# Transposing attention's result by DMA instead of TensorE for six of sixteen tiles of a fused attention and MLP block

## The chip, the cores and the metric

The kernel runs on one core of a Trainium2 chip. Its metric is the device time of one execution in microseconds (us); a time is the median of several runs. The core's engines each run their own queue of instructions in order: TensorE (PE in the profile, with its weight loads as PEld), VectorE (DVE), ScalarE (ACT), GpSimd (POOL) and SyncE (SP), which here mostly issues DMA transfers. They wait for each other by semaphores.

## What is computed

One transformer block in fp32 on a sequence of 2048 positions with 512 features: layer norm, attention with 32 heads of 16 features over a dilated window (8 keys, two positions apart), output projection and residual; then layer norm, an MLP with 1792 hidden features and squared ReLU, and residual.

```python
def _A_ref(x, wqkv, wo):
    qkv = (x @ wqkv).reshape(B, S, 3, H, Dh) ...
    idx = pos[:, None] - off[None, :]          # off = 0, 2, ..., 14
    logits = einsum("bhsd,bhswd->bhsw", q, k[idx]) * Dh ** -0.5
    attn = softmax(where(idx >= 0, logits, -1e9))
    o = einsum("bhsw,bhswd->bhsd", attn, v[idx])
    return o.transpose(0, 2, 1, 3).reshape(B, S, D) @ wo

def _B_ref(x, w1, b1, w2, b2):
    h = x @ w1 + b1
    r = where(h > 0, h, 0)
    return (r * r) @ w2 + b2

h = x + _A_ref(_layernorm(x), wqkv, wo)
h2 = h + _B_ref(_layernorm(h), w1, b1, w2, b2)
```

## The kernel before

**Tiles and groups.** The 2048 positions are 16 tiles of 128 positions, one per partition. Four tiles (R = 4) make a group, two (RI = 2) a sub-group of the attention. Tile t belongs to group t // 4 and to sub-group t // 2. Every fp32 matrix product is made of three products of parts: a number is split into a high part (a copy in the reduced fp32r type, made by ScalarE in `hi`, L141) and a low part (the difference, made by VectorE or GpSimd in `lo`, L144), and high x high, low x high and high x low are summed in PSUM.

**Phases.** A first phase makes q, k and v for all tiles and stores them in a scratch tensor in DRAM, and prepares group 0. Then come three loops, u = 0, 1, 2, each of which runs the MLP of group u and, woven into it, the preparation of group u + 1. A last stage runs the MLP of group 3 in another form.

**A loop's slots.** A loop has 17 slots, p = 0 to 16. In slot p TensorE computes one block of 128 hidden features of the four tiles (`mlp1`, 12 matmuls, L224) and the second product of the block of three slots before (`mlp2`, 12 matmuls, L808). The hidden block goes from PSUM through ScalarE (ReLU L784, square L785, high part `rh` L141) and GpSimd or VectorE (low part `rl` L144) before `mlp2` uses it. In loop 0 each slot also loads one block of w2, splits it (`big_h`, `big_l`) and stores its low half to DRAM (`stash`); in loops 1 and 2 low halves are fetched back (`fetch`).

**Preparation of a tile of the next group.** For tile t = 4(u + 1) + i, tables give the slots: LH loads the residual row h; OP = 6, 7, 12, 13 is the slot of `o_T`; WP = 8, 9, 13, 14 (one earlier for i = 2, 3 in loop u = 2) that of the product with wo. `o_T` runs at the slot's start: four TensorE transposes of 128 x 128 against an identity (`tr<-ident,o`, L199) into one PSUM bank, and at the slot's end the high part `oh` by ScalarE and the low part `ol` by VectorE, both read from PSUM. `wo_product` makes 12 matmuls (`wo<-wo_h,oh` and so on, L224); then `h_add` adds the residual and takes the statistics (VectorE L577, L152, L153), GpSimd computes the norm's scale (`rs`, L158 to L162), ScalarE normalizes (`hn`, L194), GpSimd adds b2 (L587) and SyncE stores h. At the loop's end, slots 15 and 16 (halves of slots 14 and 15 in loop 2), `hn` of the four tiles is transposed by TensorE (`tr<-ident,hn`, L199); the next loop's first product needs all four.

**Attention.** The attention of a sub-group is a generator of steps: VectorE multiplies q with a window of k (`dots`, L335) and sums (L369), ScalarE copies q to PSUM (`qp`, L264) and exponentiates (`ex`, L392), VectorE weighs v (`weigh`, L346), GpSimd adds up the products in a tree into `o` (L403). Its k, v and q windows are loaded by SyncE (L243, L256).

**Order.** The program text is emitted in one pass, and each engine runs its own instructions in the order of emission. A planner keeps two estimated clocks, one for TensorE and one for VectorE. At each slot's end `end_slot` adds the slot's TensorE time, runs the chores due (`at`), draws attention steps from the generator (`pump`) until VectorE's clock has caught up, and runs the late chores (`after`). `pump(until=s)` draws steps until sub-group s is done. Row buffers of 2 KB per partition come from one shared pool of ROWS = 15, taken in turn; a new user waits for the last reader of the old one.

Of the kernel before, what the change touches and what calls it, by code (L numbers as in the profile page):

```python
# [7 lines left out]

F32 = mybir.dt.float32
F32R = mybir.dt.float32r  # L10
AF = mybir.ActivationFunctionType
ALU = mybir.AluOpType
X = mybir.AxisListType.X

S, D, H, DH, W, F = 2048, 512, 32, 16, 8, 1792
P = 128
KB = D // P
FB = F // P
R = 4
RI = 2  # L20
# [17 lines left out]
W2 = (18,)  # L38
LH = 3, 4, 10, 11
OP = 6, 7, 12, 13  # L40
WP = 8, 9, 13, 14
HP = 15, 15, 16, 16
UP = 14, 14, 15, 15
HL = (14, 0), (14, 1), (15, 0), (15, 1)
# [8 lines left out]
def block_kernel(ctx, tc, x, wqkv, wo, w1, b1, w2, b2, out):  # L53
    nc = tc.nc
# [31 lines left out]

    big_h = wpool.tile([P, 3 * KB, D], F32R, name="big_h")
    big_l = wpool.tile([P, 3 * KB, D], F32R, name="big_l")
    wq_h, wq_l = [t.rearrange("p (k c) n -> p k (c n)", k=KB) for t in (big_h, big_l)]
    wo_h = wpool.tile([P, KB, D], F32R, name="wo_h")  # L90
    wo_l = wpool.tile([P, KB, D], F32R, name="wo_l")
    w1_h = wpool.tile([P, KB, F], F32R, name="w1_h")
    w1_l = wpool.tile([P, KB, F], F32R, name="w1_l")
    w2_h, w2_l = {}, {}

    def row(name, shape=(P, D), dt=F32):
        return work.tile(list(shape), dt, name=name, tag="row", bufs=ROWS)
# [8 lines left out]
    def at(delta, fn, *a):  # L106
        due.setdefault(now["slot"] + delta, []).append((fn, a))
# [11 lines left out]
    def run(chores):  # L119
        todo = chores.get(now["slot"], [])  # L120
        while todo:
            fn, a = todo.pop(0)
            fn(*a)

    def dve(t):
        now["dve"] += t
# [13 lines left out]
    def hi(dst, src):  # L140
        nc.scalar.copy(dst, src)  # L141

    def lo(eng, dst, src, h):
        eng.tensor_tensor(out=dst, in0=src, in1=h, op=ALU.subtract)  # L144
# [3 lines left out]
    def norm_stats(key, src, delay=True):  # L148
        st = small.tile([P, 6], F32, name="st")
        mv = small.tile([P, 2], F32, name="mv", bufs=4)  # L150
        rs = small.tile([P, 2], F32, name="rs", bufs=4)
        nc.vector.bn_stats(st, src)  # L152
        nc.vector.bn_aggr(mv, st)  # L153
        dve(0.93)
        stats[key] = mv, rs

        def finish():
            nc.gpsimd.tensor_scalar(out=rs[:, 1:2], in0=mv[:, 1:2], scalar1=EPS, scalar2=None,  # L158
                                    op0=ALU.add)
            nc.gpsimd.tensor_tensor(out=rs[:, 0:1], in0=rs[:, 1:2], in1=mhalf, op=ALU.pow)  # L160
            if delay:
                nc.gpsimd.tensor_scalar(out=rs[:, 1:2], in0=mv[:, 0:1], scalar1=rs[:, 0:1],  # L162
                                        scalar2=-1.0, op0=ALU.mult, op1=ALU.mult)
        if delay:
            after(0, finish)
        else:
            finish()

    def act_stats(key, src):
# [4 lines left out]
        scrap = row("scrap")  # L174
        nc.scalar.activation(scrap, src, AF.Identity, accum_out=nm[:, 0:1])
        nc.scalar.activation(nm[:, 1:2], nm[:, 0:1], AF.Identity, scale=-1.0 / D)
        nc.scalar.activation(scrap, src, AF.Square, bias=nm[:, 1:2], accum_out=sq)
        stats[key] = nm, rs
# [8 lines left out]
    def norm_apply(key, dst, src, eng):  # L187
# [5 lines left out]
        else:  # L193
            nc.scalar.activation(dst, src, AF.Identity, scale=rs[:, 0:1], bias=rs[:, 1:2])  # L194

# [7 lines left out]
    def parts(tr, dst):  # L203
        n = len(dst)
        return [(dst[i], tr[:, i * KB // n:(i + 1) * KB // n]) for i in range(n)]

    def hi_T(tr, h_dst):
        for d, src in parts(tr, h_dst):
            hi(d, src)

    def lo_T(tr, h_dst, l_dst):
        for (d, src), h in zip(parts(tr, l_dst), h_dst):
            lo(nc.vector, d, src, h)
            dve(0.16 + 0.53 / len(h_dst))
# [16 lines left out]
    o_t = {}  # L231
# [35 lines left out]
    def attention():  # L267
# [39 lines left out]
        for n in range(N + 1):  # L307
# [77 lines left out]
            if new:  # L385
# [5 lines left out]
                yield 0.42 + 0.15 * ng  # L391
                nc.scalar.activation(lf, lf, AF.Exp, scale=DH ** -0.5)  # L392

# [4 lines left out]
    def add_up(p2, o, c0, s):  # L398
        w = W // 2
        while w:  # L400
            dst = p2[:, :, :w] if w > 1 else o[:, :, c0:c0 + GC].rearrange(
                "p i (w h d) -> p i w h d", w=1, h=GH)
            nc.gpsimd.tensor_tensor(out=dst, in0=p2[:, :, :w], in1=p2[:, :, w:2 * w], op=ALU.add)  # L403
            w //= 2
        done[s] += 1
# [3 lines left out]
    def pump(until=None):  # L409

        while (done[until] < G) if until is not None else (now["dve"] < now["pe"]):
            todo = sums[:]
            sums.clear()
            t = next(stream, "end")
            for a in todo:
                add_up(*a)
            if t == "end":
                now["dve"] = 1e9
                return
            if t is None:  # L420
                now["dve"] = max(now["dve"], now["pe"])
                return
            dve(t * SLOW[min(now['sub'] + 1, 2)])
# [128 lines left out]
    oT = {}  # L552
# [9 lines left out]
    def o_T(t):  # L562
# [9 lines left out]
        at(0, hi_T, tr, [oT[t][0]])  # L572
        at(0, lo_T, tr, [oT[t][0]], [oT[t][1]])

    def h_add(t, ps):
        h = hs[t]
        nc.vector.tensor_tensor(out=h, in0=ps, in1=h, op=ALU.add)  # L577
        dve(0.7)
        norm_stats(t, h)
# [168 lines left out]
    def products_b(n):  # L748
# [6 lines left out]
        tt = nc.vector.tensor_tensor  # L755
        nc.scalar.activation(rf[:, :HD], b[1], AF.Relu, bias=b1_sb[:, f:f + 1])
        tt(out=u[:, HD:], in0=b[2], in1=p[:, :HD], op=ALU.add)
# [131 lines left out]
    for n in range(16):  # L889
        gp, t = divmod(n, 4)  # L890
# [66 lines left out]
    def load_w2(f):  # L957
        raws[f] = row("raw2")
        nc.sync.dma_start(raws[f], w2[f * P:(f + 1) * P, :])
# [37 lines left out]
    for u in range(R - 1):  # L997
        now["sub"] = u
        first, end = u == 0, False
        fs = list(range(FB)) if first else [*sorted(place), 12, 13]  # L1000
        fs += [f for f in range(12) if f not in fs and (u < 2 or f not in ENDS)]
        fs += ENDS if u == 2 else []
        need = [] if first else [f for f in fs if f < 12 and f not in place]
        acc = [psum.tile([P, D], F32, name="acc", tag=tag) for tag in ("acc0", "acc1", "tr0", "tr1")]
        js = range(R)


        todo, halves = {}, {}
        for i in js:
            t = R * (u + 1) + i  # L1010
            if not end:
                a = i // 2 if u == 2 else 0
                for p, *what in ((LH[i] - a, at, 0, load_h, t), (OP[i] - a, o_T, t),
                                 (WP[i] - a, wo_product, t, (0, 1, 2 + 3 * a, 3 + 3 * a))):
                    todo.setdefault(p, []).append(what)
                p, h = (HP[i], i % 2) if u < 2 else HL[i]
                (todo, halves)[h].setdefault(p, []).append((h_T, t))
            todo.setdefault(UP[i], []).append((at, 0, unspill, R * u + i))
        if u == 2:
            for p, *what in ((12, at, 0, t_load, 0), (12, at, 0, t_load, 1), (13, after, 0, t_sums, 0),  # L1020
                             (13, after, 0, t_sums, 1), (13, at, 1, t_split, 0),
                             (14, after, 0, t_split, 1)):
                todo.setdefault(p, []).append(what)

        def half(p):
            run(due)
            for fn, *a in halves[p]:
                fn(*a)

        for p in range(FB + LAG):  # L1030
            more = 0.0
            if p == FB:
                run(due)
                dve(HOLD)
            if u < 2 and p == FB - 2:
                dve(HOLD)
            for fn, *a in sorted(todo.get(p, []), key=lambda x: x[0] is wo_product):
                fn(*a)
                more += 2.73 if fn is wo_product else 0.0
            if p < FB:  # L1040
                mlp1(u, fs[p])
                more += 2.73
                if first:
                    at(0, split_w2, p)
                    if p + 1 < FB:
                        load_w2(p + 1)
            q = p - LAG
            if q >= 0:
                f = fs[q]
                mlp2(u, f, acc, js, q == 0, q == FB - 1,  # L1050
                     (lambda: half(p)) if p in halves else None)
                more += 2.74
                if f < 12 and (need or first and p < FB - LAG):
                    free.append(place.pop(f))
                    if need:
                        at(1, fetch, need.pop(0))
            end_slot(more)
        for i in js:
            at(u // 2, finish, R * u + i, acc[i])
# [83 lines left out]
```

## Time and profile before

| | before |
|---|---|
| runs | 514.01, 515.54, 515.64 us, median 515.54 |
| profiled execution, first to last instruction | 513.0 us |
| mean granted TensorE clock | 1.000 |
| PE busy | 506.4 us, 99% |
| DVE busy | 376.7 us, 73% |
| POOL busy | 350.0 us, 68% |
| ACT busy | 256.2 us, 50% |
| transposes of o on TensorE (L199) | 64, 9.6 us busy |
| share of PE in the chain that ended last | 92% |

The profile is of one execution; its time as a run is not listed apart from the three above. In the profile a line such as L199 is a line of the kernel's text; where a helper makes the instruction, as `transposes` or `hi` do, the tile names (out<-in) tell the uses apart. PE's busy time counts overlapping matmuls by their modelled ends, so that what a group of matmuls takes is read from the starts of the groups around it.

### The profile page before, as it was taken

Reading aid. Unit: us, or ns where it says so; the run is one execution under the profiler, and the core shown is the slowest. Engines: PE = TensorE matmul, PEld = TensorE weight load, DVE = VectorE, ACT = ScalarE, POOL = GpSimd, SP = SyncE. Lnnn points to the kernel's source line nnn. Section 1 sums busy time; section 2 is a strip of 40 time slices with the busy share of each in tenths; the row PEclk is TensorE's granted clock in tenths of the full one; section 3 lists DMA queues with packets and bytes.
Section 4 is the critical chain, followed back from the end, with each engine's and each line's share of the span. In section 5 each row is a group of like instructions: output and inputs, shape, how many; then the busy total and the mean of one; then the engine's idle time right before and its main releaser. Section 6 shows DMA issues by size and latency. Waiting matters only on the chain.

```text
span 513.0 us, 7625 instructions
## 1 busy us (share of the span) xinstructions
PE 506.4 (99%) x2508; PEld 429.3 (84%) x2508; DVE 376.7 (73%) x524; ACT 256.2 (50%) x498; POOL 350.0 (68%) x430
## 2 busy tenths in 40 slices
PE   7999999999999999999999999999999999999997
PEld 6999788888888888888888888888888888989996
DVE  5489799988998798976889799778984035742333
ACT  4634687767424763463364334336432525666542
POOL 4714888894885895896778759676889544685520
PEclk9999999999999999999999999999999999999999
DMA  9677989889677895685487537557632352454112
GB/s 265 193 221 188 271 283 315 275 274 278 196 234 201 291 299 173 175 232 180 129 266 229 163 94 231 174 160 257 219 94 65 106 159 84 142 145 145 63 41 82
DMA packets 88239, 97.37 MB, mean 190 GB/s; under 512 B 8328, under 2 KB 56712, under 8 KB 88200
## 3 DMA queue, kind: packets, MB, share of 16 engines
q1 hardware_dynamic: 87256, 96.37, 61.4%
q10 hardware_dynamic: 944, 0.52, 0.3%
q8 instruction: 19, 0.31, 0.3%
q14 instruction: 20, 0.16, 0.1%
HBM read 72.65 MB, written 24.25 MB: 189 GB/s over the span
## 4 chain that ended last, share of the span: by engine, by line
PE 92%; POOL 3%; DMA 2%; DVE 1%; issue 1%; ACT 1%; SPq 0%; POOLq 0%; ACTq 0%
PE mm L224 45%; PE acc L808 29%; PE wo L224 9%; PE mm L731 6%; PE tr L199 4%; DMA wraw<-in_A_wqkv_dram 1%; DMA qkv_d<-y 1%; POOL pr L403 1%; POOL h L587 1%; POOL tl L144 0%; PE half L831 0%; SPq L432 0%; POOL wo_l L144 0%; DVE pr L346 0%; DVE ex L369 0%
## 5 line engine op out<-in xcount | busy, mean ns | idle before, releaser
L403 POOL TENSOR_TENSOR pr<-pr 128x512 f32<-128x512 f32 (+1 forms) x128 | 132.1, 1032 | 51.2 <-DVE pr L346 45.7
L224 PE MATMUL mm<-big_l,w_h 128*128 128x512 f32 x336 | 89.5, 392 | 0.0
L346 DVE TENSOR_TENSOR pr<-ex,v 128x1024 f32<-128x1024 f32 x64 | 78.0, 1221 | 11.6 <-POOL o L403 7.6
L335 DVE TENSOR_TENSOR pr<-qp,k 128x1024 f32<-128x1024 f32 x64 | 76.8, 1201 | 5.7 <-ACT qp L264 5.7
L369 DVE TENSOR_REDUCE ex<-pr 128x64 f32<-128x1024 f32 x64 | 78.4, 1225 | 1.8
L224 PEld LDWEIGHTS mm<-big_l,w_h 128*128 128x128 f32 x336 | 62.3, 188 | 12.8 <-DVE ol L144 0.2
L144 POOL TENSOR_TENSOR rl<-r,rh 128x512 fp32r<-128x512 f32 x42 | 55.4, 1318 | 22.5 <-ACT rh L141 22.4
L224 PE MATMUL mm<-big_h,xl 128*128 128x512 f32 (+1 forms) x208 | 55.9, 379 | 0.2 <-DVE xl L144 0.2
L224 PE MATMUL mm<-big_h,xh 128*128 128x512 f32 (+1 forms) x208 | 53.5, 378 | 0.7 <-ACT xh L141 0.7
L784 ACT ACTIVATE r<-mm,b_sb 128x512 f32<-128x512 f32 x42 | 28.8, 686 | 47.9 <-PE mm L224 46.1
L224 PE MATMUL mm<-big_l,xh 128*128 128x512 f32 (+1 forms) x208 | 52.7, 375 | 0.0
L808 PE MATMUL acc<-big_l,rh 128*128 128x512 f32 x190 | 52.7, 391 | 0.0
L808 PE MATMUL acc<-big_h,rh 128*128 128x512 f32 x190 | 52.3, 392 | 0.0
L808 PE MATMUL acc<-big_h,rl 128*128 128x512 f32 x190 | 51.8, 390 | 0.0
L493 ACT COPY y<-mm 128x512 f32<-128x512 f32 (+1 forms) x52 | 28.6, 552 | 40.0 <-PE mm L224 30.1
L224 PE MATMUL mm<-big_l,w_l 128*128 128x512 f32 x168 | 45.0, 390 | 0.0
L224 PEld LDWEIGHTS mm<-big_h,xh 128*128 128x128 f32 x208 | 37.6, 188 | 7.0 <-ACT xh L141 1.7
L224 PEld LDWEIGHTS mm<-big_l,xh 128*128 128x128 f32 x208 | 38.2, 188 | 6.0
L224 PEld LDWEIGHTS mm<-big_h,xl 128*128 128x128 f32 x208 | 37.2, 188 | 5.7 <-DVE xl L144 0.6
L808 PEld LDWEIGHTS acc<-big_h,rl 128*128 128x128 f32 x190 | 35.7, 188 | 7.5
L808 PEld LDWEIGHTS acc<-big_l,rh 128*128 128x128 f32 x190 | 35.4, 188 | 7.3
L808 PEld LDWEIGHTS acc<-big_h,rh 128*128 128x128 f32 x190 | 34.8, 188 | 6.5
(148 smaller groups left out, 879.8 us busy)
## 6 DMA issues: line engine op xcount, KB each, us to landing
k<-qkv_d SPq DMA_DIRECT2D x48, 288.0 KB, 2.8
v<-qkv_d SPq DMA_DIRECT2D x48, 288.0 KB, 4.0
qkv_d<-y SPq DMA_DIRECT2D x18, 512.0 KB, 4.3
big_l<-w2l_d SPq DMA_DIRECT2D x24, 256.0 KB, 3.1
xt<-in_A_x_dram SPq DMA_DIRECT2D x16, 256.0 KB, 4.3
q<-qkv_d SPq DMA_DIRECT2D x32, 128.0 KB, 3.0
h<-in_A_x_dram SPq DMA_DIRECT2D x16, 256.0 KB, 4.1
h_d<-h SPq DMA_DIRECT2D x16, 256.0 KB, 4.1
```

The source lines that it names most:

```text
L144: eng.tensor_tensor(out=dst, in0=src, in1=h, op=ALU.subtract)
L199: nc.tensor.transpose(tr[:, k, :], src[:, k * P:(k + 1) * P], ident)
L224: nc.tensor.matmul(ps, l(k), r(k), start=(n == 0), stop=(n == 3 * KB - 1))
L335: nc.vector.tensor_tensor(out=pr.rearrange("p i w h d -> p i w (h d)"), in0=qps["now"][:, j % 2].unsqueeze(2).to_broadcast([P, RI, W, GC]) ...
L346: nc.vector.tensor_tensor(out=p2, in1=vwin, op=ALU.mult, in0=e1[:, :, :, j * GH:(j + 1) * GH].unsqueeze(4).to_broadcast([P, RI, W, GH, DH]))
L369: nc.vector.tensor_reduce(out=lf[:, :, :, j * GH:(j + 1) * GH], in_=pr, axis=X, op=ALU.add)
L403: nc.gpsimd.tensor_tensor(out=dst, in0=p2[:, :, :w], in1=p2[:, :, w:2 * w], op=ALU.add)
L493: nc.scalar.copy(y[:, :, t % RI * GC:(t % RI + 1) * GC], ps[:, :j * GC].rearrange("p (j c) -> p j c", j=j))
L587: nc.gpsimd.tensor_tensor(out=h, in0=h, in1=b2_sb, op=ALU.add)
L731: nc.tensor.matmul(ps, sta[y][:, k], mov[x][:, k], start=(first and q == 0), stop=(last and q == len(terms) - 1), skip_group_check=True)
L784: nc.scalar.activation(r, ps, AF.Relu, bias=b1_sb[:, f:f + 1])
L808: nc.tensor.matmul(acc[j], l[:, j * P:(j + 1) * P], w[f], start=(first and n < len(js)), stop=(last and n >= len(terms) - len(js)))
```

## The change

For the tiles with i < RI, that is tiles 4, 5, 8, 9, 12 and 13, `o_T` is replaced by three steps in consecutive slots, each at its slot's end. In slot OP (6, 7), `o_planes` draws attention until the sub-group is done, and ScalarE copies o, read as 128 x 1024 16-bit numbers, into two planes: the first halves of all 512 numbers, then the second halves. In slot OP + 1 (7, 8), `o_turn` has SyncE issue one transposing DMA of both planes, eight blocks of 128 x 128. In slot OP + 2 (8, 9), `o_join` has ScalarE copy the 16-bit numbers together again into a row of fp32, and from that row ScalarE makes `oh` and VectorE `ol`. The wo product of these tiles moves from slots 8, 9 to 9, 10. Each tile uses three more row buffers (`pl`, `ft`, `of`). Tiles 0 to 3 and the tiles with i = 2, 3 are as before. TensorE makes 24 transposes fewer; ScalarE makes 12 copies more and SyncE issues 6 transfers more. The planner's estimate of TensorE's time no longer gets the 0.44 us of a tile's transposes in these slots.

```diff
+U16 = mybir.dt.uint16
...
-WP = 8, 9, 13, 14
+WP = 9, 10, 13, 14
...
+    planes, flat = {}, {}
+
+    def halves_of(a):
+        return a.bitcast(U16).rearrange("p (n two) -> p n two", two=2)
+
+    def o_planes(t):
+        s, j = divmod(t, RI)
+        pump(until=s)
+        planes[t] = row("pl", (P, 2, D), U16)
+        nc.scalar.copy(planes[t].rearrange("p two n -> p n two"), halves_of(o_t[s][:, j, :]))
+
+    def o_turn(t):
+        flat[t] = row("ft", (P, 2, KB, P), U16)
+        nc.sync.dma_start_transpose(flat[t].rearrange("p two k c -> p (two k) c"),
+                                    planes.pop(t).rearrange("p two n -> p (two n)"))
+
+    def o_join(t):
+        tr = row("of")
+        nc.scalar.copy(halves_of(tr), flat.pop(t).rearrange("p two k c -> p (k c) two"))
+        oT[t] = row("oh", (P, KB, P), F32R), row("ol", (P, KB, P), F32R)
+        tr = tr.rearrange("p (k c) -> p k c", k=KB)
+        hi_T(tr, [oT[t][0]])
+        lo_T(tr, [oT[t][0]], [oT[t][1]])
...
-                for p, *what in ((LH[i] - a, at, 0, load_h, t), (OP[i] - a, o_T, t),
+                if i < RI:
+                    turned = ((OP[i] - a, at, 0, o_planes, t), (OP[i] + 1 - a, at, 0, o_turn, t),
+                              (OP[i] + 2 - a, at, 0, o_join, t))
+                else:
+                    turned = (OP[i] - a, o_T, t),
+                for p, *what in ((LH[i] - a, at, 0, load_h, t), *turned,
                                  (WP[i] - a, wo_product, t, (0, 1, 2 + 3 * a, 3 + 3 * a))):
```

## The prediction

> **What bounds the kernel now.** I read the page's busy shares first, then the chain that ended last, then the groups of TensorE by shape, then the timeline of TensorE in one slot with the transposes and one without. Columns of the timeline: start us, length us, engine, line, operation, tiles, count, and in brackets the idle time before with what ended it.
>
> ```profile
> span 513.0 us, 7625 instructions
> ...
> PE 506.4 (99%) x2508; PEld 429.3 (84%) x2508; DVE 376.7 (73%) x524; ACT 256.2 (50%) x498; POOL 350.0 (68%) x430
> ...
> PE   7999999999999999999999999999999999999997
> ...
> PE 92%; POOL 3%; DMA 2%; DVE 1%; issue 1%; ACT 1%; SPq 0%; POOLq 0%; ACTq 0%
> ```
>
> TensorE is busy in every slice and carries 92% of the chain. The reader is to see that a TensorE instruction taken away is worth its time only as long as nothing else turns out to be late.
>
> ```profile
> L199 PE MATMUL tr<-ident,o 128*128 128x128 f32 x64 | 9.6, 271 | 0.0
> ```
>
> These 64 are four per tile for 16 tiles; the change takes 24 away. Their 271 ns overlap in the pipeline, so the price comes from the starts (a row's count is that of the stretch looked at, not of all that follow):
>
> ```profile
> 181.86 1.07 PE L224 MATMUL mm<-big_l,w_h 128*128 128x512 f32 x4
> ...
> 187.30 0.60 PE L199 MATMUL tr<-ident,o 128*128 128x128 f32 x4
> ...
> 193.22 0.60 PE L199 MATMUL tr<-ident,o 128*128 128x128 f32 x4
> ...
> 199.15 1.07 PE L224 MATMUL wo<-wo_h,oh 128*128 128x512 f32 x4
> ...
> 207.31 1.07 PE L224 MATMUL wo<-wo_h,oh 128*128 128x512 f32 x4
> ...
> 278.48 0.49 PE L199 MATMUL tr<-ident,o 128*128 128x128 f32 x3
> ...
> 290.32 0.61 PE L224 MATMUL wo<-wo_h,oh 128*128 128x512 f32 x2
> ...
> 369.34 0.49 PE L199 MATMUL tr<-ident,o 128*128 128x128 f32 x3
> ...
> 381.18 0.61 PE L224 MATMUL wo<-wo_h,oh 128*128 128x512 f32 x2
> ```
>
> **Removed from TensorE.** Slot 5 of group 0's loop, without transposes, lasts 187.30 - 181.86 = 5.44 us. Slots 6 and 7, with them, last 199.15 - 187.30 = 11.85 us for the two; in the next two loops the pair lasts 290.32 - 278.48 = 11.84 and 381.18 - 369.34 = 11.84. Three pairs are 35.53 us against 6 x 5.44 = 32.64: **-2.89 us**, or 0.48 a tile, 0.96 a group. It is a saving on the path, since TensorE does not idle there. The other TensorE work of the slots stays; the wo products of these tiles only come one slot later.
>
> **Added, the DMA.** Per tile one transposing transfer of 128 x 1024 16-bit numbers, 256 KB. No such transfer is in the trace. The nearest rows are other transfers of 256 KB (line, count, KB, median us from issue to landing):
>
> ```profile
> out_dram<-h SPq DMA_DIRECT2D x15, 256.0 KB, 2.7
> raw<-in_B_w_dram SPq DMA_DIRECT2D x14, 256.0 KB, 5.8
> b_sb<-in_B_b_dram SPq DMA_DIRECT2D x1, 256.0 KB, 6.3
> ```
>
> So 2.7 to 6.3 us; I take 4.3, near the middle, for the landing L. What hides it is the distance that the change leaves. SyncE issues it behind the other transfers of its slot: the first behind the stash of w2's low half, the second behind the next stash, in the next loops behind a fetch:
>
> ```profile
> 194.94 0.32 SPq L989 DMA_DIRECT2D w2l_d<-big_l  x1
> ...
> 201.27 0.38 SPq L989 DMA_DIRECT2D w2l_d<-big_l  x1
> ...
> 284.38 0.38 SPq L994 DMA_DIRECT2D big_l<-w2l_d  x1
> ```
>
> and ScalarE copies beside it cost:
>
> ```profile
> 187.94 0.59 ACT L141 CAST oh<-tr 128x512 fp32r<-128x512 f32 x1 [1.09 <-PE tr L199]
> 189.24 0.62 ACT L141 CAST big_h<-raw 128x512 fp32r<-128x512 f32 x1 [0.72 <-DMA raw<-in_B_w_dram]
> 189.77 0.37 ACT L264 COPY qp<-q 128x256 f32<-128x256 f32 x1
> ...
> 192.14 0.63 ACT L141 CAST rh<-r 128x512 fp32r<-128x512 f32 x1
> ...
> 204.85 0.69 ACT L784 ACTIVATE r<-mm,b_sb 128x512 f32<-128x512 f32 x1 [3.82 <-PE mm L224]
> ```
>
> **Added, ScalarE.** Twelve copies of 1024 numbers: 256 cost 0.37 and 512 cost 0.62, 0.25 per 256, so 1.12 us by extension. Bounds: 0.62 (as a 512 copy of the same bytes) to 2.5 (four of these, if 16-bit numbers at a stride go at half the rate); I take 1.1, because count, not bytes, ties the two rows. That is 13 us on an engine that is busy 50%. The split stands where the hi copy stood: that copy ends a 1.09 us idle wait for TensorE's transposes, which falls away, so the split mostly uses that hole, and the 3.82 us hole before the ReLU at 204.85 takes what is over. Behind it in ScalarE's order stand the high half of the next w2 block, a qp copy or an exponent; without the hole each would be up to 1.1 us late and VectorE's dots with them, which is the second rival's ground and not TensorE's path at once.
>
> The joined result for tile 4: issue 194.94 + 0.32 = 195.26, plus 4.3 = 199.6, join to 200.7, high half (0.62) to 201.3, and VectorE's low half about 0.7 later. The wo product now starts at slot 9, 187.30 + 3 x 5.44 = 203.62: it is in time while L is under 203.62 - 195.26 - 1.72 = **6.6 us**. For tile 5 the issue is at 201.65 and wo starts a slot of 207.31 - 199.15 = 8.16 later, at 211.78: L under 8.4. For tile 8: issue 284.76, wo at 278.48 + 16.32 = 294.80, L under 8.3. Group 3 has group 1's shape, and I give it the 6.6 of tile 4. With copies at 2.5 these shrink by 1.4, still above my L; with 2.5 and 6.3 together, tiles 4 and 12 miss by 1.1 each. I take **0** for the sum and **+2.2** for its upper end. Below nothing it cannot go: a product in time gains nothing by being earlier.
>
> [...]
>
> The call that drives attention up to the sub-group moves from a slot's start to its end; it forces nothing new, since the o that it asks for was transposed at that slot's start before. Six more issues on SyncE at 0.3 to 0.4 us each lie in a queue that TensorE does not wait for; in group 0's loop a k, a q and a k load stand behind each. Three more row buffers per tile out of 15 are taken in turn; the next user of the planes' buffer (a low half of the hidden block, on GpSimd) waits for the landing, two slots before TensorE multiplies it: 0 while L is under a slot, 5.44.
>
> **Where the saved time meets other work.** The transposes of h at a loop's end wait for GpSimd's work on the norm, which is queued between attention's sums. Group 1's last tile:
>
> ```profile
> 240.76 2.11 POOL L403 TENSOR_TENSOR pr<-pr 128x512 f32<-128x512 f32 x2 [3.50 <-DVE pr L346]
> ...
> 247.19 2.13 POOL L403 TENSOR_TENSOR pr<-pr 128x512 f32<-128x512 f32 x2
> ...
> 250.93 0.27 POOL L162 TENSOR_SCALAR rs<-mv,rs 128x1 f32<-128x1 f32 x1
> ```
> ```profile
> 251.23 0.82 ACT L194 ACTIVATE hn<-h,rs 128x512 f32<-128x512 f32 x1 [1.57 <-POOL rs L162]
> ```
> ```profile
> 250.46 1.63 PE L808 MATMUL acc<-w_x,rh 128*128 128x512 f32 x6
> 252.10 0.65 PE L199 MATMUL tr<-ident,hn 128*128 128x128 f32 x4
> ```
>
> hn is ready at 252.05 and the transposes start at 252.10, while six matmuls at 0.227 (5.44 / 24) from 250.46 are done at 251.82: TensorE already waits 0.28 us here. GpSimd works without a gap from 240.76 to this rs, and what started it there was a product of VectorE, which queues behind the h_add of tile 6:
>
> ```profile
> 235.67 0.69 DVE L577 TENSOR_TENSOR h<-wo,h 128x512 f32<-128x512 f32 x1 [0.33 <-PE wo L224]
> ...
> 239.46 1.22 DVE L346 TENSOR_TENSOR pr<-ex,v 128x1024 f32<-128x1024 f32 x1
> ```
>
> That h_add moves up 0.96 with TensorE. But the planner counts 0.44 us of TensorE per tile's transposes as time to fill, and without them one weighted product that stood ahead of this h_add now stands behind it, in front of the one at 239.46: 1.22 - 0.96 = 0.26 later for it and for the sums on GpSimd up to rs. So TensorE, 0.96 early, waits 0.96 + 0.26 longer: **+1.22** given back. Bounds: -0.28 (even the old wait goes, if the product is done in VectorE's idle time) to 0.96 + 1.22 = 2.18 (if the h_add does not move up). In group 2:
>
> ```profile
> 315.41 0.47 POOL L403 TENSOR_TENSOR o<-pr 128x128 f32<-128x128 f32 x1
> ```
> ```profile
> 290.84 0.37 ACT L392 ACTIVATE ex<-ex 128x256 f32<-128x256 f32 x1 [4.93 <-DVE ex L388]
> 341.15 0.82 ACT L194 ACTIVATE hn<-h,rs 128x512 f32<-128x512 f32 x1 [0.51 <-POOL rs L162]
> ```
> ```profile
> 317.52 0.60 PE L199 MATMUL tr<-ident,o 128*128 128x128 f32 x4
> 343.02 0.60 PE L199 MATMUL tr<-ident,hn 128*128 128x128 f32 x4
> ```
>
> The exponent now stands behind tile 8's join: 284.76 + 4.3 + 1.72 = 290.8, so it starts about where it did, and moves one for one with any longer L. Tile 10's o is ready at 315.88, its transposes at 317.52 move up 0.96: slack 0.68, less an attention lag of up to 1.0. Bounds 0 to 1.3; I take **+0.3**. The last h transpose has 343.02 - 341.97 = 1.05 of slack and keeps its 0.96. Group 3:
>
> ```profile
> 394.33 0.47 POOL L403 TENSOR_TENSOR o<-pr 128x128 f32<-128x128 f32 x1
> ```
> ```profile
> 402.94 0.60 PE L199 MATMUL tr<-ident,o 128*128 128x128 f32 x4
> ```
>
> attention's last sum ends 8.1 us before tile 14's transposes, so group 3 keeps all of its 0.96.
>
> Sum: -2.89 + 0 + 1.22 + 0.30 = **-1.37 us**. The profiled span of 513.0 goes to 511.6. The span lies 2.54 below the median of the three runs, 515.54, which covers start and end outside the trace; the change touches neither, so the time is 515.54 - 1.37 = **514.17**. A measurement here can tell about 0.3%, 1.55 us, from no change.
>
> **Rivals.** First, all is hidden: 515.54 - 2.89 = 512.65. For it speaks TensorE's idle of 0.0 before the removed rows; against it the 0.28 us wait at 252.10, which has no reserve.
>
> Second, attention falls behind: the joins sit ahead of exponents on ScalarE and VectorE's low halves, which wait for a DMA, ahead of attention's reductions. With the upper ends 2.18 at the tail and 1.3 at tile 10 the sum is +0.6: 516.1. For it speaks GpSimd's gapless stretch; against it the 3.82 us ScalarE hole and a VectorE that is busy 73%.
>
> Third, the other side, slower: the transfer is served in pieces one behind another, and the wo products wait for the join. Four pieces at the shortest row, 2.7, are 10.8 us: tile 4 is late by 4.2, tile 8 by 2.5, tile 12 by 4.2, the second tile of each group by nothing further, as TensorE has slipped. -2.89 + 10.9 = +8.0: **523.5**; tail waits vanish in it. It breaks even near L = 8.1 and is slower by 0.3% from about 8.7. [...] For it: the distances of 6.6 to 8.4 us are no more than the longest row plus a little. Against it: no 256 KB row above 6.3.
>
> **How the numbers follow.** Forecast 0.38 (513.2 to 515.2); all hidden 0.19; attention behind 0.12; serial transfer 0.31. Faster by over 0.3% (under 513.99) takes all hidden and about half of the forecast's case: 0.36. Slower (over 517.09): the serial case and a corner of attention behind, 0.34. Within: 0.30. Of the serial case a part, L of 8.7 to 10, ends at 517 to 521. The range 512.2 to 520.5 leaves out some 0.05 below and 0.15 above; the likeliest case's own is 513.2 to 515.2.
>
> **What would show it.** Right: 40 transposes of o instead of 64; slots 6 to 8 of the three loops near 5.44; wo of tile 4 at 203.6 with no idle before it; transfers landing in 3 to 6 us; the last h transpose of group 1 still near 252.1 to 252.4, with a longer wait for hn. Wrong: landings above 6.6 and TensorE idle before wo on oh or ol; copies of 1024 above 2 us; idle of over 1 us before tile 10's transposes; or the wait near 252 not growing, which would make it the first rival.

## The result, and the profile after

The changed kernel takes 528.32 us (median of 5 runs, 527.20 to 531.10) against 515.25 for the kernel before beside it: a ratio of 1.0266, with a 95% interval of 1.0250 to 1.0282. It is 13 us slower. The forecast was 514.17 us, with 520.5 as the upper end of its range.

The page of the changed kernel, the lines that answer to those of before:

```profile
span 526.2 us, 7601 instructions
PE 509.0 (97%) x2484; PEld 429.4 (82%) x2484; DVE 377.8 (72%) x524; ACT 291.2 (55%) x510; POOL 349.9 (66%) x430
PE   7999999999999999989899997999998999999997
PE 28%; POOL 7%; DVE 2%; ACT 2%; issue 1%; POOLq 0%; ACTq 0%
```

TensorE is now under 90% busy in slices 18, 20, 25 and 31 of the 40. (The chain that ended last is followed back only in part here: its shares add up to 40%, so that they cannot be held against the 92% of before.) ScalarE is busy 35 us longer, where 13 were planned. Which of the three new operations that is, the views of their tiles tell (count, then shortest, median and longest duration in ns, first and last start):

```profile
L585 ACT COPY pl<-o x6: 4881/4914/4952, 186.6 to 385.9; 128x1024 uint16<-128x1024 uint16 x6
L589 SPq DMA_TRANSPOSE ft<-pl x6: 1237/1368/1810, 193.1 to 393.4; - x6
DMA to landing us min/median/max: 3.6/4.1/4.6
```
```profile
L594 ACT COPY of<-ft x6: 1157/1168/1173, 201.4 to 399.6; 128x1024 uint16<-128x1024 uint16 x6
```

The DMA lands in 4.1 us, where 4.3 was assumed, and the join takes 1.17, where 1.1 was. The split, a copy of the same count and type as the join, takes 4.91 us, twice its upper bound of 2.5. And the DMA holds SyncE for 1.24 to 1.81 us an issue, where 0.3 to 0.4 was assumed.

TensorE's waits, from the view of waits (us in total, times, longest). The kernel before had only the waits for mhalf (1.3), xt (1.1) and xh (0.7) and 0.2 us more:

```profile
PE tr L200 <- POOL o L404: 3.4, 1, 3.4
PE tr L200 <- ACT hn L195: 2.4, 2, 1.8
PE wo L225 <- ACT oh L142: 2.0, 1, 2.0
PE mm L225 <- ACT r L809: 1.8, 1, 1.8
PE tr L881 <- POOL mhalf L867: 1.3, 1, 1.3
PE wo L225 <- DVE h L602: 1.0, 1, 1.0
PE mm L225 <- ACT xh L142: 0.7, 1, 0.7
PE tr L200 <- DVE xt L191: 0.6, 1, 0.6
```

The eight rows are 13.2 us; with 0.4 for a low half and 0.2 in the last stage they make 13.8, against 3.3 before. The largest falls on tile 10, one of the tiles that still go by TensorE, so there it is attention that is late. How that comes about can be read in loop 1 of the changed kernel. ScalarE:

```profile
281.83 4.88 ACT L585 COPY pl<-o 128x1024 uint16<-128x1024 uint16 x1
286.20 0.78 ACT L265 COPY qp<-q 128x256 f32<-128x256 f32 x1
...
288.82 4.95 ACT L585 COPY pl<-o 128x1024 uint16<-128x1024 uint16 x1
...
297.06 1.17 ACT L594 COPY of<-ft 128x1024 uint16<-128x1024 uint16 x1 [1.08 <-DMA ft<-pl]
298.31 0.62 ACT L142 CAST oh<-of 128x512 fp32r<-128x512 f32 x1
298.84 0.37 ACT L393 ACTIVATE ex<-ex 128x256 f32<-128x256 f32 x1
```

VectorE, SyncE's queue, then TensorE in the same loop:

```profile
287.01 1.23 DVE L336 TENSOR_TENSOR pr<-qp,k 128x1024 f32<-128x1024 f32 x1 [4.55 <-ACT qp L265]
...
290.54 1.22 DVE L336 TENSOR_TENSOR pr<-qp,k 128x1024 f32<-128x1024 f32 x1
...
298.96 1.53 DVE L145 TENSOR_TENSOR ol<-of,oh 128x512 fp32r<-128x512 f32 x1 [2.28 <-ACT oh L142]
```
```profile
291.78 0.32 SPq L244 DMA_DIRECT2D k<-qkv_d  x1
...
292.63 1.81 SPq L589 DMA_TRANSPOSE ft<-pl  x1
```
```profile
325.45 0.33 PE L200 MATMUL tr<-ident,o 128*128 128x128 f32 x1 [3.41 <-POOL o L404]
```

A q copy of attention stands behind the first split, and VectorE's dots wait 4.55 us for it. The next dots end at 291.76, and the k load that reuses their window goes out at 291.78; the transposing DMA, behind it and a fetch in SyncE's queue, is issued at 292.63, though its planes were done at 286.7 and 284.76 was expected. So the join is late, VectorE's low half waits another 2.28 us with attention queued behind it, and the exponent runs at 298.84, where before it ran at 290.84. Some 26 us later TensorE stands for 3.41 us until GpSimd has tile 10's o.

The waits are not the whole price. The view of stretches (TensorE's granted clock is the third number from the right) for two stretches just behind waits of 3.41 and 1.97 us:

```profile
325.45:330.00 4.55, 4.55 (x14) 3.60 (x15) 3.44 (x5) 0.96 (x2) 3.57 (x3) 0.62 0.51 158
...
397.85:402.50 4.65, 4.65 (x13) 3.67 (x14) 3.72 (x5) 3.47 (x5) 1.78 (x2) 0.63 0.16 41
```

Over these 4.6 us the clock is 0.62 and 0.63 on average. The twelve matmuls that start at 325.54 last until the next start at 329.96, 4.42 us, and the twelve from 397.85 to 402.30 last 4.45, where twelve of the same size take 2.72 from 407.77 to 410.49 of the same run: 1.7 us more a time. So 13.8 - 3.3 = 10.5 us more waiting, 3.4 of slower matmuls and -2.89 of transposes make +11.0 of the 13.2 by which the span grew. Where the other 2.2 lie was not followed.

### The profile page after: what moved, and what is told of

It reads as the page before. It is cut to its first block, busy times and chain, and to the rows that moved or that the text cites. A ratio compares the mean times of both kernels' runs of the same rounds, so it can differ in the third digit from the quotient of the medians.

```text
span 526.2 us, 7601 instructions
## 1 busy us (share of the span) xinstructions
PE 509.0 (97%) x2484; PEld 429.4 (82%) x2484; DVE 377.8 (72%) x524; ACT 291.2 (55%) x510; POOL 349.9 (66%) x430
## 5 line engine op out<-in xcount | busy, mean ns | idle before, releaser
L225 PEld LDWEIGHTS mm<-big_l,w_h 128*128 128x128 f32 x336 | 63.5, 190 | 15.2 <-ACT r L809 2.0
```

What stands on the lines that cost most here:

```text
L225: nc.tensor.matmul(ps, l(k), r(k), start=(n == 0), stop=(n == 3 * KB - 1))
```

## The experiments

Times are medians of the runs of each kernel; the kernel before ran beside them each time (medians of 514.77 to 515.35), and the ratio with its 95% interval is against that.

### Split walked plane by plane

```diff
-        nc.scalar.copy(planes[t].rearrange("p two n -> p n two"), halves_of(o_t[s][:, j, :]))
+        nc.scalar.copy(planes[t], halves_of(o_t[s][:, j, :]).rearrange("p n two -> p two n"))
```

> The changed kernel with one edit: the split into planes walks all first halves, then all second halves, instead of alternating between the planes number by number. Same instruction count, same DMAs, same order. Theory (the split's alternating writes are what costs): the split falls from 4.91 us to 1.2 us, as the join costs, ScalarE is no longer late, TensorE's waits fall from 13.8 us to under 5, and the time is 512.5 to 514.5 us. Rival 1 (the transposing DMA and the 1.2 to 1.8 us that it holds SyncE cause the delay): the DMA is unchanged, so the time stays above 524. Rival 2 (16-bit numbers cost ScalarE 4.9 us in any order when an fp32 row is read at a stride): split stays at 4.9 us, time 528.

```profile
L585 ACT COPY pl<-o x6: 1039/1042/1042, 186.9 to 376.2; 128x1024 uint16<-128x1024 uint16 x6
```
```profile
PE tr L200 <- ACT hn L195: 2.4, 2, 1.8
...
PE tr L200 <- POOL o L404: 1.1, 1, 1.1
```

The split falls from 4.91 to 1.04 us and the time from 528.32 to **516.38** (1.0026, 1.0015 to 1.0037). The DMA, with its 1.24 to 2.23 us on SyncE, is still there, so rivals 1 and 2 fall. The theory is right on the split and misses its own range by 2 us: TensorE's waits fall to 7.1 us, not under 5, and the kernel is still slower than before. The rows above say where: TensorE waits for tile 7's hn and tile 10's o, the two places that the prediction had named, and for tile 11's hn, where it had counted on 1.05 us of slack.

### Join walked plane by plane too

```diff
-        nc.scalar.copy(halves_of(tr), flat.pop(t).rearrange("p two k c -> p (k c) two"))
+        nc.scalar.copy(halves_of(tr).rearrange("p n two -> p two n"),
+                       flat.pop(t).rearrange("p two k c -> p two (k c)"))
```

> As the split by plane, and the join is walked plane by plane as well, so that now the join writes 16-bit numbers 4 bytes apart and reads them in order. Theory, if steps between writes are what costs: the join goes from 1.17 us up towards 4.9 and stands before the wo product, time 516 to 528. If only steps over a larger distance (from one plane to the other, 1 KB) cost, the join stays near 1.2 us and the time is that of the split by plane within 0.3%.

```profile
L594 ACT COPY of<-ft x6: 1357/1371/1372, 198.0 to 388.3; 128x1024 uint16<-128x1024 uint16 x6
```

516.85 us (1.0030, 1.0019 to 1.0041). Writing 16-bit numbers 4 bytes apart takes 1.37 us, writing them in order while reading from alternating planes takes 1.17. What takes 4.91 is writes that alternate between places 1 KB apart. Why they take that long was not shown, and other distances were not tried.

### Split alone, slow and fast

```diff
+    def o_planes(t):
+        s, j = divmod(t, RI)
+        pl = row("pl", (P, 2, D), U16)
+        nc.scalar.copy(pl.rearrange("p two n -> p n two"), halves_of(o_t[s][:, j, :]))
...
+                if i < RI:
+                    todo.setdefault(OP[i] - a, []).append((at, 0, o_planes, t))
```

> The kernel before, with TensorE's transposes kept and used, plus the six alternating splits at the place where the change puts them; the planes are not used, and there is no DMA and no join. Theory: 4.9 us of ScalarE in front of the exponents and q copies of attention and of the hidden block's parts is the whole loss, so the time rises by 8 to 16 us, to 523 to 531. Rival 1 (the DMA is to blame): 515 to 517.

> As the kernel before with six splits added, but these walk plane by plane. Theory: 1.2 us each fit in ScalarE's idle time, 515 to 516.5 us. Rival 2 (any split of 16-bit numbers is slow): 523 to 531, like the alternating one.

The slow one takes 518.05 us (1.0057, 1.0043 to 1.0071), the fast one 515.57 (1.0018, 0.9999 to 1.0036). The fast one is as its theory had it. The slow split is there in full (4.94 us), and yet it costs 2.9 us, not 8 to 16, between the ranges of theory and rival. This theory falls: the length of the split alone is not the loss. In the kernel before the split stands behind the high half of its own tile, and the slots' attention steps are in another order.

### Wo products one slot later, alone

```diff
-WP = 8, 9, 13, 14
+WP = 9, 10, 13, 14
```

> The kernel before with the wo products of the six tiles one slot later (slots 9 and 10 in place of 8 and 9) and nothing else: TensorE's transposes stay, no split, DMA or join. Theory that order matters at the groups' ends: the later h_add shifts attention's steps and the time moves by 0.3 to 1.5 us, to 515.4 to 516.6. Rival (the slot is free): 515.1 within 0.3.

514.98 us (0.9994, 0.9984 to 1.0003): the slot is free, and the rival holds.

### The whole chain, read by nobody

The kernel before, with split, DMA and join added as in the change; TensorE's transposes and wo stay as before.

```diff
...
+    def o_join(t):
+        tr = row("of")
+        nc.scalar.copy(halves_of(tr), flat.pop(t).rearrange("p two k c -> p (k c) two"))
...
```

> The kernel before with TensorE's transposes kept and used, wo at its old slots, plus the alternating split, the transposing DMA and the join in the change's slots; the joined row is read by nobody. Against the split alone (518.05) it adds the DMA, SyncE's hold and a join on ScalarE that waits for the landing with exponents and q copies behind it. Theory A (attention stands behind splits and joins, and its late o is what TensorE waits for): 521 to 529. Theory B (the loss needs the wo product to wait for the join): 517.5 to 519.

518.35 us (1.0060, 1.0047 to 1.0074), as much as the slow split alone. DMA, SyncE's hold and the join's place on ScalarE cost nothing that can be told; theory A falls in this form, and the time lies in theory B's range. But here nothing on VectorE, attention's engine, waits for the chain either, so the next run adds that.

### The whole chain, with a low half

```diff
+        oh2, ol2 = row("oh2", (P, KB, P), F32R), row("ol2", (P, KB, P), F32R)
+        hi_T(tr, [oh2])
+        lo_T(tr, [oh2], [ol2])
```

> The kernel before with TensorE's transposes used, plus the alternating split, DMA and join as in the run of the whole unused chain (518.35), and now also a high half by ScalarE and a low half by VectorE made from the joined row, which nobody reads. Theory (VectorE's low half waits for ScalarE's two slow splits and the join, and attention, queued behind it on VectorE, is what gets late): VectorE's waits for ScalarE rise from 18.6 to over 25 us and the time to 521 to 529, though TensorE needs nothing of the chain. Rival (only the wo product that waits for the join makes the loss): 518 to 519.5.

```profile
PE tr L200 <- POOL o L404: 7.9, 2, 5.7
PE mm L225 <- ACT r L808: 4.8, 5, 2.4
```

**535.99** us (1.0410, 1.0396 to 1.0424): twelve short instructions more, whose result nobody reads, cost 17.6 us. TensorE needs nothing of the chain here, and it waits for attention's o and for ReLUs. That the wo product must wait is not needed for a loss, so the rival, and with it theory B of the run before, falls. But the time lies above the theory's range too, and the edit does three things at once: VectorE gets an instruction that waits for the chain; the planner counts its 0.7 us, so that attention's steps move as well; and each tile takes two more of the 15 row buffers. The last shows in GpSimd's waits: its low half of the hidden block waits 4.3 us (three times) for the join, which it does in neither the change nor the run before. How much each of the three costs, these runs do not show. VectorE's waits for ScalarE (high half, q copy, exponent, from 180 to 425 us) are 24.7 us here, 18.6 in the run before, 31.8 in the change and 10.1 in the kernel before; the theory asked for over 25. This sum is higher in the change than here, though the change is 8 us faster, so it does not measure the loss by itself.

### Slow split behind the slot's attention steps

```diff
-                    turned = ((OP[i] - a, at, 0, o_planes, t), (OP[i] + 1 - a, at, 0, o_turn, t),
+                    turned = ((OP[i] - a, after, 0, o_planes, t), (OP[i] + 1 - a, at, 0, o_turn, t),
```

> The changed kernel with its alternating split of 4.9 us, emitted after the slot's attention steps instead of before them, so that on ScalarE the q copies, exponents and w2 high halves of the same slot stand ahead of it. The other engines' orders are unchanged. Theory (the loss comes from q copies behind the split: VectorE waits 4.55 us for one of them, its k loads go late on SyncE's queue and the transposing DMA is queued behind them): the time falls from 528 to 517 to 522. Rival (the split's length delays the next ReLU and the join as much from any place): 525 or more.

525.81 us (1.0200, 1.0183 to 1.0217): the theory's 517 to 522 is missed, the rival's 525 or more holds. VectorE's waits, from 180 to 425 us, in the change and then in this run:

```profile
DVE ol L145 <- ACT oh L142: 17.5, 7, 5.0
DVE pr L336 <- ACT qp L265: 8.8, 3, 4.6
...
DVE sm L359 <- ACT ex L393: 5.5, 2, 5.1
```
```profile
DVE ol L145 <- ACT oh L142: 26.3, 6, 7.9
...
DVE sm L359 <- ACT ex L393: 2.7, 2, 2.2
...
DVE pr L336 <- ACT qp L265: 0.8, 1, 0.8
```

The wait for the q copy is gone as meant (8.8 to 0.8), but VectorE now waits for the high half, 26.3 instead of 17.5 us; the sum only goes from 31.8 to 29.8. With the splits later, the join and its high half are later, and the low half stands at the same place in VectorE's queue. So not the q copy alone was the trouble.

### Old planner estimate; DMA in the split's slot; both

All three with the split by plane. First, the planner keeps the 0.44 us:

```diff
+    def pe(t):
+        now["pe"] += t
...
+                if i < RI:
+                    todo.setdefault(OP[i] - a, []).append((pe, 0.44))
```

> The split by plane, and the planner's TensorE estimate keeps the 0.44 us per tile in slots 6 and 7 that TensorE's transposes had, so that attention's weighted products stand ahead of h_add again as in the kernel before. No instruction is added. Theory (what the split by plane still loses is VectorE's and GpSimd's order at the groups' ends): TensorE's waits for hn (2.4 us) and o (1.1 us) fall by 1 to 2 us together, time 514 to 515.4 against 516.4. Rival (attention is late because ScalarE and the queue have more to do, whatever the order): 516.0 to 516.8.

516.77 us (1.0032, 1.0020 to 1.0045), not faster than the 516.38 of the split by plane and in the rival's range. Yet TensorE's waits for hn and o are gone, as the theory said, and two waits for ReLUs, 2.3 us together, came in their place. VectorE, ScalarE (the join of tile 5 and a later exponent) and TensorE in loop 0 of this run:

```profile
210.15 0.69 DVE L148 TENSOR_TENSOR ol<-of,oh 128x512 fp32r<-128x512 f32 x1 [5.65 <-ACT oh L145]
```
```profile
208.24 1.17 ACT L597 COPY of<-ft 128x1024 uint16<-128x1024 uint16 x1 [2.25 <-DMA ft<-pl]
...
222.85 0.37 ACT L396 ACTIVATE ex<-ex 128x256 f32<-128x256 f32 x1 [6.55 <-DVE ex L392]
```
```profile
228.10 1.90 PE L228 MATMUL mm<-big_l,w_h 128*128 128x512 f32 x4 [1.97 <-ACT r L812]
```

The low half of tile 5 comes earlier in VectorE's order and waits 5.65 us, since the join before it waits for a DMA that has not landed. Attention is late behind it, an exponent on ScalarE waits 6.55 us for VectorE, ReLUs stand behind that exponent, and TensorE waits 1.97 us for the second of them. So the DMA was moved up:

```diff
-                    turned = ((OP[i] - a, at, 0, o_planes, t), (OP[i] + 1 - a, at, 0, o_turn, t),
+                    turned = ((OP[i] - a, at, 0, o_planes, t), (OP[i] - a, at, 0, o_turn, t),
```

> The split by plane with the transposing DMA issued in the split's own slot, one slot earlier on SyncE's queue; the join stays where it is, and no other engine's order changes. Theory (the second tile's DMA of a pair is late because it stands behind loads that wait, and VectorE's low half waits for the join with attention behind it): VectorE's and ScalarE's waits for the join vanish, 515.0 to 516.0 against 516.4. Rival (the landing is hidden anyway, the group ends decide): 516.2 to 516.8.

> As the last one, and with the planner's 0.44 us per tile kept, as in the run with the old estimate (516.8). There VectorE waited 5.65 us for the low half of the second tile behind a DMA that landed late. Theory: with the DMA a slot earlier that wait and the later wait of TensorE for a ReLU (2.0 us) go, 513.8 to 515.3. Rival: no change, 516.5 to 517.

The earlier DMA alone gives 516.74 us (1.0034, 1.0020 to 1.0048): no change. Its rival holds: TensorE's waits for hn (2.4 us) and o (1.1 us), at the groups' ends, are as they were. Both together give **511.94** us (0.9940, 0.9927 to 0.9954), faster than before by 3.4 and faster than the theory's 513.8 to 515.3. The low half of tile 5 in this run, and tile 7's h at the end of group 1:

```profile
205.37 0.69 DVE L148 TENSOR_TENSOR ol<-of,oh 128x512 fp32r<-128x512 f32 x1 [1.42 <-ACT oh L145]
```
```profile
250.69 0.66 PE L203 MATMUL tr<-ident,hn 128*128 128x128 f32 x4
```

5.65 us have become 1.42, and tile 7's h is transposed at 250.69 (252.10 before, 256.00 in the change). No wait of TensorE is left in the three loops that its view of waits lists, and the span is 509.9, 3.1 less than before; 0.43 of that was gained ahead of the loops (155.09 against 155.52 below), which the edits do not touch.

### That order with the slow split

```diff
-        nc.scalar.copy(planes[t], halves_of(o_t[s][:, j, :]).rearrange("p n two -> p two n"))
+        nc.scalar.copy(planes[t].rearrange("p two n -> p n two"), halves_of(o_t[s][:, j, :]))
```

> The order that gave 511.94 (old estimate, DMA in the split's slot, split by plane) with the alternating split of 4.9 us put back and nothing else changed. Theory (split's length decides, order only the last few us): 519 to 527. Rival (the order was the fault and the length is hidden in it): 512 to 515.

515.45 us (1.0018, 1.0006 to 1.0030). The theory falls and the rival is nearly right: in this order the slow split costs 3.5 us, not 12. With the change's order and this one (planner's 0.44 us kept and DMA a slot earlier, together), fast and slow, four runs stand in a square: 516.38 and 528.32 in the change's order, 511.94 and 515.45 in this. The slow split costs 11.9 us in the first and 3.5 in the second; the change's order costs 4.4 us more than this one with the fast split and 12.9 with the slow one. (By the ratios to the kernel before, which ran beside each, they are 12.4 and 4.0, 4.4 and 12.8.) Neither alone is the cause: of the 16.4 us between the fastest and the slowest of the four, 8.4 come only where both meet.

### The last group without TensorE's transposes of o

```diff
+TP = 6, 7, 9, 10
...
+                wp = WP[i] if u == 2 or i >= RI else WP[i] - 1
+                if u == 2:
+                    turned = ((TP[i], at, 0, o_planes, t), (TP[i] + 1, at, 0, o_turn, t),
+                              (TP[i] + 2, at, 0, o_join, t))
...
```

> The split by plane with DMA and join for all four tiles of group 3 alone (tiles 14 and 15 with their planes in slots 9 and 10); groups 1 and 2 as in the kernel before, wo at its old slots there. Theory: attention is over in that loop, so nothing gives TensorE's four times 0.48 us back: 515.1 - 1.9 = 513.2 us, range 512.8 to 514.2. Rival (joins or the wo products of this loop wait as well): 515 or more.

513.95 us (0.9977, 0.9968 to 0.9986), 1.3 us of the expected 1.9 gained, within the theory's range. The same for tiles 14 and 15, with the DMA in the split's slot, added to the best order:

> The order that gave 511.94 with the split by plane, and in the last of the three loops the other two tiles of group 3 go by DMA too (planes in slots 9 and 10). Theory (TensorE's 0.48 us a tile is kept in full where no attention follows): 511.94 - 0.96 = 511.0, range 510.5 to 511.6. Rival (the joins collide there): 511.8 or more.

511.80 us (0.9938, 0.9925 to 0.9950). Within the intervals it is the same as 511.94, just at the edge of the rival's range; if the two tiles add anything, these runs do not show it.

## Why the prediction was wrong

**What held.** Slots 6 to 8 of loop 0 last (203.43 - 187.11) / 3 = 5.44 us each, as forecast, and the wo product of tile 4 starts at 203.43 without a wait (203.6 forecast):

```profile
187.11 1.07 PE L225 MATMUL mm<-big_l,w_h 128*128 128x512 f32 x4
...
203.43 1.09 PE L225 MATMUL wo<-wo_h,oh 128*128 128x512 f32 x4
```

The -2.89 is real: in the best order it is kept in full, from the first transposes of h to the last, in the kernel before and then in that run:

```profile
155.52 1.03 PE L199 MATMUL tr<-ident,hn 128*128 128x128 f32 x8
...
431.16 0.60 PE L638 MATMUL tr<-ident,hn 128*128 128x128 f32 x4
```
```profile
155.09 1.03 PE L203 MATMUL tr<-ident,hn 128*128 128x128 f32 x8
...
427.81 0.60 PE L666 MATMUL tr<-ident,hn 128*128 128x128 f32 x4
```

275.64 us have become 272.72, 2.92 less. The landing (4.1 for 4.3), the join (1.17 for 1.1) and the free slot for wo held too. That the landing came so near is partly luck: it was the middle of rows of other transfers, and over all runs it lay between 2.7 and 7.6 us. That a transfer is served in four pieces one behind another was the author's supposition, and no run shows it; the six landings took 3.6 to 4.6 us, where it had 10.8, so the third rival was nearest in time (523.5) but not in cause. The hold of SyncE's queue was put at 0.3 to 0.4 us an issue and is 1.24 or more; the split by plane, which keeps that hold, shows that it is not what cost the 12 us.

**The step that failed first: the split's size.** "256 cost 0.37 and 512 cost 0.62, 0.25 per 256, so 1.12 us by extension", with 2.5 as the upper end. Both rows write in order. The split writes alternately to two planes, and no row of the trace had such a write; the text bounded it by half a rate, an assumption that no row showed. It measured 4.91, and with the planes walked one after the other 1.04. In the change's order that one edit takes back 11.9 us. The prediction had listed copies above 2 us, and over 1 us of idle time before tile 10's transposes, as signs of being wrong; both came.

**The step that failed with it: where the late work meets the path.** "Each would be up to 1.1 us late ... which is the second rival's ground and not TensorE's path at once." The second rival, attention behind, was the mechanism, and it was priced by its ends at the groups' tails, 516.1 us. What it lacked is that attention goes round, as the rows of loop 1 show: ScalarE's split holds VectorE's dots, these hold the k loads in SyncE's queue, these hold the transposing DMA, and that comes back as VectorE's low half. A piece that is late by 4 us meets itself again, and tile 10 pays. That the split and the order make the loss together is shown by the four runs; this path from one to the other is read from the trace, and the runs that cut into it support it only in part: without anything on VectorE that waits for the chain 518.35, with it 535.99 (and two other things changed), with the q copy's wait taken out still 525.81. The matmuls behind two of the waits, where the clock is 0.62 and 0.63, take 1.7 us more a time; the prediction had no term for it.

**A size that was too small: what the groups' ends give back.** With the split repaired, the sum can be held against the trace. TensorE there, at the last transposes of groups 1, 2 and 3:

```profile
252.94 0.66 PE L200 MATMUL tr<-ident,hn 128*128 128x128 f32 x4 [1.79 <-ACT hn L195]
...
344.97 0.66 PE L200 MATMUL tr<-ident,hn 128*128 128x128 f32 x4 [0.56 <-ACT hn L195]
...
432.21 0.60 PE L663 MATMUL tr<-ident,hn 128*128 128x128 f32 x4
```

Tile 7's h comes at 252.94 for 252.10 before, from loops that began 0.1 us later (155.63 for 155.52), so group 1 gives back 0.96 + 0.74 = 1.70, where 1.22 was forecast. Tile 11's comes at 344.97 for 343.02, so group 2 gives back 0.96 + 1.11 = 2.07, where 0.30 was; tile 10's wait of 1.12 alone is near the upper end of 1.3, and tile 11's 0.56 was not in the sum. Group 3 goes from 88.14 us (431.16 - 343.02) to 87.24 and keeps 0.90. The mechanism was the one named: with the old estimate the waits at tiles 7, 10 and 11 go. With these two sizes the sum is -2.89 + 1.70 + 2.07 = +0.9 us, where -1.37 was forecast; the span grew by 1.3. But the old estimate's order paid only with the DMA a slot earlier.

## What to carry to other kernels

A copy's price can depend on the order in which it writes (4.91 against 1.04 us here), so take it only from a row that walks the same way; before accepting a strided copy, walk the other side in order. An in-order engine that is half idle (ScalarE, busy 55% of the span in the changed kernel) still is on the path if a chain of other engines' queues comes back to it: follow what a new wait holds, on every queue, until it meets itself. When a planner's estimate is part of the order, an instruction taken away changes the order of others; keep the estimate and move the instruction separately, and try the two together, since either alone showed nothing here (516.8 and 516.7) and both gave 511.9.

## What the runs showed of the hardware

- Writes of 16-bit numbers by ScalarE that alternate between places 1 KB apart: 4.91 us for 1024 a partition. The same numbers plane by plane 1.04; written 4 bytes apart 1.37; read alternately and written in order 1.17.
- TensorE's granted clock fell to 0.50 at the end of some waits or just behind: in the change it is 0.50 from 326.4 to 329.6 and from 398.0 to 401.4, which makes the 0.62 and 0.63 of the longer stretches above, with waits of 3.41 and 1.97 us there. Behind a wait of 1.97 in the run with the old estimate it is 0.61 on average from 228.1 to 232.5, and behind one of 5.72 in the whole chain with a low half 0.57 from 327.7 to 333.0. In the run with the slow split behind attention's steps, four matmuls take 1.71 us behind a wait of 1.82 (starts at 258.61 and 260.32) and 1.85 behind one of 2.23 (325.95 and 327.80), where four take 0.91 elsewhere. The clock stayed at 1.00 behind a wait of 1.80 us, at 256.00 in the change, and behind one of 3.03 us with the slow split behind attention's steps four matmuls take 1.03 (399.12 to 400.15) and the next four 0.91:

```profile
256.00:261.00 5.00, 5.00 (x24) 4.22 (x25) 4.35 (x9) 1.25 (x5) 1.57 (x2) 1.00 0.17 62
```
```profile
399.12 1.20 PE L225 MATMUL wo<-wo_h,oh 128*128 128x512 f32 x4 [3.03 <-ACT oh L142]
```

So by the length of the wait alone the two kinds are not told apart: a wait of 1.82 us had slower matmuls behind it, and one of 3.03 had not. What decides it was not shown.

- A transposing DMA of 256 KB from SBUF to SBUF held SyncE's queue for 1.24 to 2.23 us an issue, where plain transfers of that size in the changed kernel have medians of 0.34 to 0.53 by tile and line (a single one, of b2, took 2.20), and landed 2.7 to 7.6 us after it, over all runs that had it.
